# Four small pads that shift tiles within the partition, and three steps moved in a slot table: a fused attention, dense layer and expert router

## Chip, cores and metric
The kernel runs on one core of one Trainium2 chip, as one launch. The metric is the device time of an execution in microseconds (us), the median of several runs.

## What is computed
Linear attention over q, k, v (8 batches, 8 heads, 576 positions, 64 features), a dense layer pair, then a mixture of 8 experts with one expert for each of the 4608 tokens:

```python
q_s = softmax(q, axis=-1); k_s = softmax(k, axis=2)      # k: over the positions
kv  = einsum('bhsd,bhse->bhde', k_s, v)
x   = einsum('bhsd,bhde->bhse', q_s, kv)                 # -> [4608, 512]
h = x @ w_in;  x = (h - tanh(h)) @ w_out                 # 512 -> 2048 -> 512
logits = normed(x) @ normed(expert_emb).T / tau          # 8 experts
e = argmax(logits); gate = softmax(logits)[e]
out = gate * (relu(x @ w1[e]) @ w2[e])                   # 512 -> 1024 -> 512
```

## The kernel before
Work is tiled over tokens in 9 blocks of 512. A block of the dense layers is 16 slots, one for each 128 of the 2048 hidden features, so there are 144 slots. In each slot TensorE (PE) runs 12 matmuls of 512 columns for the first layer (`l1`, line 627, into `hps`) and 12 for the second layer of two slots earlier (`l2`, line 680, into four accumulators `acc`). There are three products for each factor pair, since every fp32 operand is split into a high and a low part: weights `wih`, `wil` (pools `wina`, `winb`) and `woh`, `wol` (pool `wout`), attention output `xth`, `xtl` (pool `xt`), activations `gh`, `gl` (pool `g`). In `l1` the weights are the stationary operand (`lhsT`, loaded by LDWEIGHTS, the rows of PEld) and x streams as the moving operand; in `l2` the activations are stationary and the weights stream.

Between the two, ACT and VectorE (DVE) compute the activation (`gfn`, lines 639 to 641 and 243) and split it (`gsplit`, lines 661 to 665). `hps` has two buffers, so `l1` of a slot needs the first DVE operation of `gfn` (`gg<-hps,gt`) of two slots before.

What else is computed during block j goes into the same slots: k of batch j+1 (class `KUnit`, four pairs of heads p = 0 to 3, each with `mx` the row maxima on DVE, line 363; `red` the maximum over partitions on GpSimd (POOL), line 369, result `mb`; `sub` on DVE, line 381; `exp` on ACT, line 387; `kv` on PE, line 393, result `pk`), q of block j+1 (`QBlock`, lines 543 to 574, partly on POOL as `stq<-stq,...`), and the router of block j-1 (`Router`: logits by 32 DVE products, `soft`, the one-hot `roh`, `rank` on PE at line 787, `fin` on DVE at lines 796 to 819, `scatter` of the rows to DRAM by four DMAs that POOL issues, line 825).

The order on every engine is written out by hand: `at(slot, order, step)` files a step under a slot and a fraction, and `run_slot` emits the steps of a slot by that fraction. Each engine then runs its own instructions in that order, and semaphores between engines do the rest. In a slot, `l1` stands at 0.30, `gfn` at 0.50, `l2` at 0.70, a router product at 0.85, `gsplit` at 0.90. So a step's fraction says what it stands behind on its engine.

After the 144 slots come units of tokens that share an expert: 16 "pair" units of 256 tokens (first layer at line 1131, 96 matmuls of 256 columns each, split as above; second layer at line 1167, 48 matmuls of 512 columns) and then units of 128 tokens.

**Where the tiles lie.** Tiles of a pool lie one behind the other in each partition, in bytes of 4 per fp32 element, and the pools on the left lie one behind the other in the order in which they are opened: `const`, `xt`, `g`, `attn`, `wout`, `wina`. In the built program of before, `const` ends at byte 7072, which is 416 modulo 512. The tiles of `xt` and `g` have sizes that are multiples of 512, so x and the activations start at 416 modulo 512. The tiles of `attn` have not, and the weights of `wout` and `wina` start at 0. The distance of the next stationary operand from the streaming one, modulo 512, is 96 in `l1` and 416 in `l2`. In the expert units the second layer has both operands in one pool, at a distance of 0; in the first layer the distance is 0 in even units (x and weights in the pool `moe2a`, on the right) and 384 in odd ones (x in the pool `moe2b`, on the left).

Of the kernel before, what the change touches and what calls it, by code (L numbers as in the profile page):

```python
# [10 lines left out]
F32 = mybir.dt.float32  # L11
# [10 lines left out]
P = 128  # L22
# [50 lines left out]
def moe_kernel(ctx, tc, q, q_t, k_t, v_t, w_in, w_out, emb, tau, w1, w2, out, dbg=None):  # L73
# [6 lines left out]
    cp = ctx.enter_context(tc.tile_pool(name="const", bufs=1))  # L80
# [4 lines left out]
    pe = nc.tensor  # L85


    ident = cp.tile([P, P], F32, name="ident")
    make_identity(nc, ident)
    ones_b = cp.tile([P, P], BF16, name="ones_b")  # L90
# [61 lines left out]
    def emb_load(xp, gp):  # L152

        em = [
            xp.tile([P, E // 2, DM], F32, name="em0", tag="stl"),
            gp.tile([P, E // 2, DM], F32, name="em1", tag="em1"),
        ]
        for i, z in enumerate(em):
            nc.sync.dma_start(
                out=z.rearrange("p e d -> p (e d)"),  # L160
                in_=emb.rearrange("(o e) d -> o (e d)", o=2)[i : i + 1].to_broadcast(
                    [P, E // 2 * DM]
                ),
            )
        return [em[e // (E // 2)][:, e % (E // 2), :] for e in range(E)]
# [14 lines left out]
    def full_run(general):  # L180
        def lpool(name, **kw):
            st = ExitStack()
            return st, st.enter_context(tc.tile_pool(name=name, bufs=1, reuse_waits="tile", **kw))
# [4 lines left out]
        wos, wop = lpool("wout")  # L188
# [6 lines left out]
        lazy = {}  # L195


        win_h, win_l, wout_h, wout_l = {}, {}, {}, {}
        raws = {}
        npair = [0]  # L200
# [115 lines left out]
        def at(slot, order, fn, *a):  # L316
            ev.setdefault(slot, []).append((order, len(ev.get(slot, ())), fn, a))
# [12 lines left out]
        class KUnit:  # L330
# [84 lines left out]
            def schedule(self, s):  # L415
                if s:
                    at(s - 2, 0.65, self.load)
                    at(s - 2, 0.66, self.loadv)
                    at(s, 0.20, self.mx)
                at(s, 0.30, self.red)  # L420
                at(s + 1, OPT['ks'] if self.b > 1 else OPT['ks1'], self.sub)
                at(s + 1, 0.85, self.exp)
                at(s + 2, OPT['kv'], self.kv)
                at(s + 2, 0.80, self.rs)
                at(s + 3, 0.20, self.out)
# [262 lines left out]
        class Router:  # L688
# [145 lines left out]
            def schedule(self, s):  # L834
                at(s, 0.75, self.evict)
                at(s, 0.98, self.ss, (0, 1))
                at(s + 1, 0.98, self.ss, (2, 3))
                ns = OPT['ns'] if self.j + 2 < NB else (4, 4, 4, 5, 5, 5, 5)
                for i, n in enumerate(ns, 1):
                    at(s + i, 0.22, self.some, n - OPT['gd'])  # L840
                    at(s + i, 0.85, self.some, OPT['gd'])
                s += len(ns)
                at(s, 0.97, self.soft)
                at(s + 1, 0.95, self.rank)
                at(s + 1, 0.97, self.fin)
                at(s + 1, 0.99, self.scatter)


        def make_table(tp, nm, nt, off, cnt, u):
# [428 lines left out]
        def open_router():  # L1278
            ds_.close()
            _, lazy["rp"] = lpool("router", side="right")  # L1280
            lazy["rps"] = _
            lazy["tp"] = lazy["rp"]
            rp = lazy["rp"]
            lazy["em"] = emb_load(xp, rp)
            lazy["ess"] = rp.tile([P, E], F32, name="ess")
            if not general:
                nc.sync.dma_start(out=taub, in_=tau.to_broadcast([P, 1]))

        at(NCH - 1, 0.99, open_router)
        for e in range(E):  # L1290
            at(
# [21 lines left out]
        def x_bufs(pool, n):  # L1313
            lazy["xg"].append(pool.tile([P, 8, P], F32, name=f"xg{n}"))

        def open_second():
            lazy["wbs"].close()
            was.close()
            lazy["sas"], lazy["sa"] = lpool("moe2a", side="right")
            for i in (1, 0):  # L1320
                u0.w1_parts(i)
            lazy["xg"] = []
            x_bufs(lazy["sa"], 0)
            u0.x_parts()
            lazy["w1t"].append(lazy["sa"].tile([P, KD, FF // 2], F32, name="w1t1"))
            u0.loadw1(1)


        u0 = units[0]
        fp = OPT['fp']  # L1330
        at(*OPT['fu'], first_unit)
        at(NS - 1, fp[0], open_second)
        at(NS - 1, fp[1], u0.split1, 0, (0,))
        at(NS - 1, fp[2], u0.split1, 0, (1,))
# [137 lines left out]
    def check(ps_m):  # L1472
# [17 lines left out]
        )  # L1490

    full_run(False)
    fv = nc.values_load(flag[0:1, 0:1], min_val=0, max_val=1)
    with tc.If(fv > 0):
        full_run(True)
# [61 lines left out]
```

## Time and profile before

| | us |
|---|---|
| median of 3 runs (lowest, highest) | 1425.31 (1424.25, 1426.81) |
| the profiled execution, its own time | 1426.07 |
| its span in the trace | 1424.4 |
| PE busy in the span | 1327.9 (93%) |
| DVE busy | 1070.3 (75%) |
| ACT busy | 786.7 (55%) |
| POOL busy | 351.4 (25%) |

An execution's own time is 1.7 us longer than its span. Busy time is the union of an engine's instructions; matmuls overlap in the pipeline, and a matmul of 512 columns has a row of about 0.40 us though the next one starts after 0.23 us. The rate of PE is therefore read from the starts of its rows in the timeline, and its waits from the view of waits.

### The profile page before, as it was taken

What the parts mean: (1) busy time and instruction counts of PE and PEld (TensorE: products, weight loads), DVE (VectorE), ACT (ScalarE), POOL (GpSimd) and SP (SyncE); (2) the same over time, 40 slices, a digit from 0 to 9 for tenths busy, and PEclk for the clock granted to TensorE, in tenths of its full rate; (3) what the DMA queues carried; (4) which work ended last, traced back from release to release, by engine and by line L of the source; (5) the groups of instructions that cost most, each with busy time, mean ns of one, the idle gap of its engine ahead of it and who ended that gap; (6) DMA issues with size and microseconds to landing.
All of it is one profiled execution on the core that took longest, in us unless ns stands there. A gap on an engine that the chain in (4) does not pass through costs nothing. (4 is left out here: it accounts for less than half of the span.)

```text
span 1424.4 us, 20194 instructions
## 1 busy us (share of the span) xinstructions
PE 1327.9 (93%) x6705; PEld 1105.3 (78%) x6705; DVE 1070.3 (75%) x2123; ACT 786.7 (55%) x1567; POOL 351.4 (25%) x335
## 2 busy tenths in 40 slices
PE   3676799999999999999999999999999899999997
PEld 2455677787787787777777787888899799989886
DVE  5788858968869779679689696777997767676453
ACT  3466555554555465564554654546554567676553
POOL 3344511112112112111121220001223343544300
PEclk9888899999999999999999999999999999999998
DMA  5454420121111210210300100005611988847784
GB/s 166 136 158 147 130 70 19 45 71 38 41 57 38 64 53 19 63 53 19 94 22 20 60 1 23 8 23 164 177 38 60 274 296 253 265 127 237 233 309 180
DMA packets 127975, 151.41 MB, mean 106 GB/s; under 512 B 52464, under 2 KB 80624, under 8 KB 127600
## 3 DMA queue, kind: packets, MB, share of 16 engines
q1 hardware_dynamic: 112800, 114.27, 26.4%
q10 hardware_dynamic: 9216, 16.78, 4.1%
q0 software_dynamic: 5840, 18.92, 3.5%
q8 instruction: 57, 0.93, 0.3%
q14 instruction: 62, 0.51, 0.1%
HBM read 164.04 MB, written 23.91 MB: 132 GB/s over the span
## 5 line engine op out<-in xcount | busy, mean ns | idle before, releaser
L680 PE MATMUL acc<-woh,gh 128*128 128x512 f32 x576 | 232.7, 404 | 0.0
L680 PE MATMUL acc<-woh,gl 128*128 128x512 f32 x576 | 229.9, 399 | 0.8 <-DVE gl L665 0.8
L680 PE MATMUL acc<-wol,gh 128*128 128x512 f32 x576 | 229.4, 398 | 0.0
L661 ACT ACTIVATE gh<-gg 128x512 fp32r<-128x512 f32 x144 | 90.9, 631 | 229.2 <-DVE gg L243 227.8
L728 DVE SCALAR_TENSOR_TENSOR rjk<-xr,em 128x512 bf16<-128x512 f32 x288 | 206.3, 731 | 3.1 <-ACT rsq L716 2.9
L627 PE MATMUL hps<-xth,wil 128*128 128x512 f32 x576 | 161.7, 403 | 35.7 <-POOL wil L297 35.7
L627 PE MATMUL hps<-xth,wih 128*128 128x512 f32 x576 | 162.8, 404 | 4.9 <-DVE gg L243 3.6
L627 PEld LDWEIGHTS hps<-xth,wil 128*128 128x128 f32 x576 | 110.3, 192 | 63.5 <-POOL wil L297 37.4
L627 PE MATMUL hps<-xtl,wih 128*128 128x512 f32 x576 | 159.1, 398 | 0.1
L639 ACT ACTIVATE gt<-hps 128x512 f32<-128x512 f32 x144 | 84.7, 588 | 91.1 <-PE hps L627 90.5
L680 PEld LDWEIGHTS acc<-woh,gl 128*128 128x128 f32 x576 | 109.3, 190 | 29.2 <-DVE gl L665 3.0
L680 PEld LDWEIGHTS acc<-woh,gh 128*128 128x128 f32 x576 | 109.8, 191 | 27.2 <-issue 0.7
L680 PEld LDWEIGHTS acc<-wol,gh 128*128 128x128 f32 x576 | 109.3, 190 | 27.6 <-issue 0.8
L627 PEld LDWEIGHTS hps<-xtl,wih 128*128 128x128 f32 x576 | 108.7, 189 | 27.5 <-DVE xtl L613 0.7
L627 PEld LDWEIGHTS hps<-xth,wih 128*128 128x128 f32 x576 | 105.3, 189 | 31.5 <-DVE gg L243 7.2
L243 DVE SCALAR_TENSOR_TENSOR gg<-hps,gt 128x512 f32<-128x512 f32 x144 | 98.1, 681 | 37.4 <-ACT gt L639 26.9
L1167 PE MATMUL po<-wl,hh 128*128 128x512 f32 x296 | 116.3, 393 | 4.2 <-DVE wl L1155 4.2
L1143 DVE SCALAR_TENSOR_TENSOR hl<-ph,hh 128x512 fp32r<-128x512 f32 x74 | 50.9, 688 | 90.7 <-ACT hh L1142 89.7
L243 DVE SCALAR_TENSOR_TENSOR gg<-gy,gg 128x512 f32<-128x512 f32 x144 | 106.2, 737 | 16.1 <-ACT gy L641 0.9
L1167 PE MATMUL po<-wh,hh 128*128 128x512 f32 x296 | 115.9, 392 | 0.0
L1167 PE MATMUL po<-wh,hl 128*128 128x512 f32 x296 | 115.4, 390 | 0.0
L665 DVE TENSOR_TENSOR gl<-gg,gh 128x512 fp32r<-128x512 f32 x132 | 95.4, 722 | 25.0 <-ACT gh L661 23.8
(266 smaller groups left out, 2527.5 us busy)
## 6 DMA issues: line engine op xcount, KB each, us to landing
w2t<-in_moe_w_dram SPq DMA_DIRECT2D x84, 512.0 KB
w1t<-in_w_t_dram SPq DMA_DIRECT2D x38, 1024.0 KB
vt<-in_v_t_dram SPq DMA_DIRECT2D x32, 325.0 KB
kt<-in_k_t_dram SPq DMA_DIRECT2D x56, 160.0 KB
gw<-in_moe_w_in_dram ACTq DMA_DIRECT2D x32, 256.0 KB
gw<-in_moe_w_out_dram ACTq DMA_DIRECT2D x32, 256.0 KB
xg<-xs_d SPq DMA_DIRECT2D x60, 128.0 KB
stq<-in_q_t_dram SPq DMA_DIRECT2D x14, 512.0 KB
```

Of the source, the lines that this page charges most:

```text
L243: dve.scalar_tensor_tensor(out=o, in0=x, scalar=s1, in1=y, op0=op0, op1=op1)
L627: pe.matmul(h, lhsT=wt[:, kk, :], rhs=xx[:, kk, :], start=(n == 0), stop=(n == 3 * KD - 1),)
L639: act(out=t, in_=h, func=AF.Square)
L661: act(out=gh, in_=g, func=AF.Copy)
L665: e.tensor_tensor(out=gl, in0=g, in1=gh.bitcast(F32), op=ALU.subtract)
L680: pe.matmul(acc[j, t], lhsT=a[:, sl], rhs=r, start=(c == 0 and i == 0), stop=(c == NCH - 1 and i == 2),)
L728: dve.scalar_tensor_tensor(out=jk, in0=self.x[t // 2][:, t % 2, 0:DM], scalar=1.0, in1=lazy["em"][e], op0=ALU.mult, op1=ALU.mult, accum_ou ...
L1143: dve.scalar_tensor_tensor(out=hl, in0=self.ph, scalar=0.0, in1=hh.bitcast(F32), op0=ALU.max, op1=ALU.subtract,)
L1167: pe.matmul(po, lhsT=a[:, f % self.wd, sl], rhs=r[:, f % 2, :], start=(f == 0 and i == 0), stop=(f == 7 and i == 2),)
```

## The change
Four tiles are allocated that nothing writes or reads: 32 bytes at the start of `const`, 416 bytes at the start of `wout`, 32 bytes at the start of the router's pool (on the right), and 192 and 320 bytes in `moe2a`, on the right. And three kinds of steps get other places: for batches 2 to 8, `mx` goes from fraction 0.20 of its slot to 0.80 of the slot before, and `red` from 0.30 to 0.01; `rank`, `fin` and `scatter` go from 0.95, 0.97 and 0.99 of a slot to 0.32, 0.33 and 0.34 of the next, which is behind that slot's `l1`.

```diff
+    cp.tile([P, 8], F32, name="pad0")
     ident = cp.tile([P, P], F32, name="ident")
...
+        wop.tile([P, 104], F32, name="pad1")
         win_h, win_l, wout_h, wout_l = {}, {}, {}, {}
...
                     at(s - 2, 0.65, self.load)
                     at(s - 2, 0.66, self.loadv)
-                    at(s, 0.20, self.mx)
-                at(s, 0.30, self.red)
+                    late = self.b < 2
+                    at(s if late else s - 1, 0.20 if late else 0.80, self.mx)
+                at(s, 0.30 if self.b < 2 else 0.01, self.red)
...
                 at(s, 0.97, self.soft)
-                at(s + 1, 0.95, self.rank)
-                at(s + 1, 0.97, self.fin)
-                at(s + 1, 0.99, self.scatter)
+                at(s + 2, 0.32, self.rank)
+                at(s + 2, 0.33, self.fin)
+                at(s + 2, 0.34, self.scatter)
...
             rp = lazy["rp"]
+            rp.tile([P, 8], F32, name="pad2")
             lazy["em"] = emb_load(xp, rp)
...
             x_bufs(lazy["sa"], 0)
+            lazy["sa"].tile([P, 48], F32, name="pad3")
             u0.x_parts()
             lazy["w1t"].append(lazy["sa"].tile([P, KD, FF // 2], F32, name="w1t1"))
             u0.loadw1(1)
+            lazy["sa"].tile([P, 80], F32, name="pad4")
```

In the built program, x and activations of the dense layers now start at 448 modulo 512, and so do their weights (0 + 32 + 416): the distance is 0 in `l1` and in `l2`. The second layer of the expert units stays at 0. In their first layer x is at 448 and the split weights are at 256, so the distance is 320 in all pair units.

On PE, near the end of a block, the rank product (`pr`, with its two weight loads) stood ahead of a slot's `l1`. Before:

```order
L393 MATMUL pk<-vt,kt 128x130 x5
L787 LDWEIGHTS tri
L787 MATMUL pr<-roh,tri 128x32
L787 LDWEIGHTS ones_b
L787 MATMUL pr<-roh,ones_b 128x32
L627 MATMUL hps<-xth,wih_1178 128x512 x4
L627 MATMUL hps<-xtl,wih_1178 128x512 x4
L627 MATMUL hps<-xth,wil_1179 128x512 x4
```

After the change:

```order
L396 MATMUL pk<-vt,kt 128x130 x5
L631 MATMUL hps<-xth,wih_1180 128x512 x4
L631 MATMUL hps<-xtl,wih_1180 128x512 x4
L631 MATMUL hps<-xth,wil_1181 128x512 x4
L791 LDWEIGHTS tri
L791 MATMUL pr<-roh,tri 128x32
L791 LDWEIGHTS ones_b
L791 MATMUL pr<-roh,ones_b 128x32
```

It moved behind the twelve matmuls of `l1`; on DVE the order of `soft` and `fin` among their neighbours is unchanged.

On POOL, over a block; `ISA mb<-mx` is the maximum over partitions, and a bare `ISA` is a change of POOL's program library between it and the `TENSOR_TENSOR` rows. Before:

```order
L369 ISA mb<-mx 128x128
L703 COPY xr<-tokid 128x2 x2
L566 ISA
L566 TENSOR_TENSOR stq<-stq,qbmax 128x512 x2
L369 ISA
L369 ISA mb<-mx 128x128
L566 ISA
L566 TENSOR_TENSOR stq<-stq,qbmax 128x512 x2
L566 TENSOR_TENSOR stq<-stq,qbadd 128x512 x2
L369 ISA
L369 ISA mb<-mx 128x128
```

After the change:

```order
L372 ISA mb<-mx 128x128
L707 COPY xr<-tokid 128x2 x2
L372 ISA mb<-mx 128x128
L570 ISA
L570 TENSOR_TENSOR stq<-stq,qbmax 128x512 x4
L570 TENSOR_TENSOR stq<-stq,qbadd 128x512 x2
L372 ISA
L372 ISA mb<-mx 128x128
```

The maximum of pair p = 1 moved ahead of the four subtractions of q, and two changes of library are gone from each such block.

On DVE, in the slot of pair p = 2's maxima. Before:

```order
L562 RECIPROCAL qbadd<-qbadd 128x64
L728 SCALAR_TENSOR_TENSOR rjk,rl<-xr,em_1414 128x512
L665 TENSOR_TENSOR gl<-gg,gh 128x512
L363 TENSOR_REDUCE mx<-kt 128x128
L728 SCALAR_TENSOR_TENSOR rjk,rl<-xr,em_1414 128x512
```

After the change:

```order
L566 RECIPROCAL qbadd<-qbadd 128x64
L366 TENSOR_REDUCE mx<-kt 128x128
L732 SCALAR_TENSOR_TENSOR rjk,rl<-xr,em_1417 128x512
L669 TENSOR_TENSOR gl<-gg,gh 128x512
L732 SCALAR_TENSOR_TENSOR rjk,rl<-xr,em_1417 128x512
```

The reduction moved two rows up, ahead of a router product and of the split of the activation.

## Rows read from the trace of the kernel before
**Rows 1.** The windows view (us, busy of each engine with instruction counts, clock, DMA share, GB/s).
```profile
0.00:165.00 165.00, 99.88 (x416) 77.89 (x417) 128.83 (x191) 81.90 (x212) 70.97 (x76) 0.85 0.48 147
...
560.00:986.00 426.00, 418.67 (x1833) 333.71 (x1832) 329.07 (x804) 227.91 (x480) 62.62 (x66) 1.00 0.14 41
986.00:1414.00 428.00, 423.83 (x2747) 385.91 (x2745) 303.84 (x419) 257.62 (x397) 140.29 (x119) 1.00 0.66 208
```

**Rows 2.** The same view for line 627 alone (PE and PEld).
```profile
165.00:986.00 821.00, 387.69 (x1562) 290.66 (x1560) 1.00 0.16 46
```

**Rows 3.** The view of waits on PE (us in total, times, longest).
```profile
PE hps L627 <- POOL wil L297: 35.7, 4, 10.3
...
PE pr L787 <- DVE roh L778: 9.4, 6, 1.7
...
PE hps L627 <- DVE gg L243: 3.6, 7, 1.0
PE pk L393 <- ACT kt L387: 3.2, 8, 0.9
```

**Rows 4.** Timeline of PE, one slot (start us, us, engine, line, operation, tiles, shape, count).
```profile
408.82 1.08 PE L627 MATMUL hps<-xth,wih 128*128 128x512 f32 x4
...
411.61 0.40 PE L680 MATMUL acc<-woh,gh 128*128 128x512 f32 x1
...
414.42 0.40 PE L627 MATMUL hps<-xth,wih 128*128 128x512 f32 x1
```

**Rows 5.** Timeline of PE, second layer of a pair unit of the experts.
```profile
1019.68 0.40 PE L1167 MATMUL po<-wh,hh 128*128 128x512 f32 x1
...
1021.75 0.39 PE L1167 MATMUL po<-wh,hh 128*128 128x512 f32 x1
...
1030.60 0.64 PE L1131 MATMUL ph<-xth,w1h 128*128 128x256 f32 x4
```

**Rows 6.** Timeline of PE, first layer of two pair units: end of an even one, start of an odd.
```profile
1042.12 0.39 PE L1167 MATMUL po<-wh,hh 128*128 128x512 f32 x1
...
1008.15 0.53 PE L1131 MATMUL ph<-xth,w1h 128*128 128x256 f32 x3
```

**Rows 7.** Timeline around the rank product, PE and DVE.
```profile
474.33 1.28 PE L393 MATMUL pk<-vt,kt 128*128 128x130 f32 x10
...
476.92 0.19 DVE L778 TENSOR_TENSOR roh<-rca,rcm 128x32 bf16<-128x32 f32 x1
...
477.17 0.19 PE L787 MATMUL pr<-roh,tri 128*128 128x32 bf16 x1 [1.56 <-DVE roh L778]
...
480.02 0.17 DVE L796 COPY rrb<-rrb 128x8 f32<-128x8 f32 x1
```

**Rows 8.** Timeline around two of k's pairs: POOL, DVE, PE.
```profile
423.73 0.72 POOL L369 PARTITION_ALL_REDUCE mb<-mx  x1 [5.71 <-issue]
...
439.53 2.76 POOL L566 TENSOR_TENSOR stq<-stq,qbadd 128x512 f32<-128x512 f32 x2 [5.67 <-DVE qbadd L562]
448.20 0.72 POOL L369 PARTITION_ALL_REDUCE mb<-mx  x1 [5.91 <-issue]
...
424.48 0.83 DVE L381 TENSOR_TENSOR kt<-kt,mb 128x640 f32<-128x640 f32 x1 [3.12 <-POOL mb L369]
...
426.13 1.39 PE L393 MATMUL pk<-vt,kt 128*128 128x130 f32 x10 [0.34 <-ACT kt L387]
...
450.60 1.38 PE L393 MATMUL pk<-vt,kt 128*128 128x130 f32 x10 [0.17 <-ACT kt L387]
```

**Rows 9.** Timeline of a wait for a first-layer accumulator: DVE, PE.
```profile
443.81 0.68 DVE L243 SCALAR_TENSOR_TENSOR gg<-hps,gt 128x512 f32<-128x512 f32 x1
...
444.55 1.21 PE L627 MATMUL hps<-xth,wih 128*128 128x512 f32 x4 [0.21 <-DVE gg L243]
```

**Rows 10.** Timeline of the next block's first pair: exponential on ACT, product on PE.
```profile
499.01 0.72 ACT L387 ACTIVATE kt<-kt 128x640 f32<-128x640 f32 x1
...
503.16 1.28 PE L393 MATMUL pk<-vt,kt 128*128 128x130 f32 x10
```


## Prediction
> **What bounds the kernel now.** I read the windows first. From 165 to 1414 us PE is the bound: in the stretches of the dense layers and of the experts it is busy for 418.67 of 426 and 423.83 of 428 us, while DVE is at 329 and 304 us, and the granted clock is 1.00 in both [rows 1]. So a nanosecond saved on PE there is a nanosecond of the run, and work of other engines counts only where PE waits for it. Before 165 us it is not so: PE is busy for 99.88 of 165 us, and four waits for decoded weights, 35.7 us in all, set the pace [rows 1, 3]. What PE saves there is waited away.
>
> Next I read how fast PE goes where it never waits. The 12 matmuls of a slot's `l1` start at 408.82 us, the 12 of `l2` at 411.61, the next slot's at 414.42: 2.79/12 = 232.5 ns and 2.81/12 = 234.2 ns for one, 5.60 us for the 24 [rows 4]. The second layer of an expert unit, with the same shapes and the same clock, does 48 in 1030.60 - 1019.68 = 10.92 us: 227.5 ns for one; its first nine take 2.07 us (230 ns), the other 39 take 8.85 us (226.9 ns) [rows 5]. Something makes each matmul of the dense layers 5 to 7 ns slower than the shape demands.
>
> Then the waits of PE. Beyond the decode they are short but regular: 9.4 us in 6 times for the one-hot ahead of the rank product, 3.6 us for the accumulator of `l1`, 3.2 us for k's exponential [rows 3].
>
> **The change part by part.**
>
> *Distances in the dense layers.* What differs between the two rates is where the operands lie: 96 and 416 in the dense layers, 0 in the experts' second layer. The change makes all of them 0. In the stretch where PE sets the pace, line 627 has 1562 recorded matmuls, which is 130 slots of 12 [rows 2]. If a slot's 24 matmuls go at 227.5 ns, they take 5.46 instead of 5.60 us, 0.14 us less: 130 x 0.14 = 18.2 us. The ends: at the 230 ns of the first nine after a break, a slot takes 5.52 us and the gain is 130 x 0.08 = 10.4 us; at 226.9 ns it takes 5.45 us, and the gain is 130 x 0.154 = 20.0 us. Dense slots have breaks too (a new accumulator every three matmuls in `l2`, k's product in one slot of four); the run of 48 has its break in its mean, so I take its 227.5 ns. As the nearest row that speaks against it: its DVE is a little less busy (71 against 77% of the stretch [rows 1]).
>
> [...]
>
> *Distances in the experts' first layer.* An even unit (distance 0) does 96 matmuls of 256 columns from 1030.60 to 1042.12 us, an odd one (384) from 1008.15 to 1019.68: 120.0 and 120.1 ns for one [rows 5, 6]. No row has 320. Bounds: the only price of a distance that rows show is the 6.7 ns between 234.2 and 227.5 [rows 4, 5]; on the 1536 matmuls of the 16 pair units that is 10.3 us, either way. Two distances that far apart read alike, so I take 0.
>
> *The rank product.* It waits at the head of PE, so all twelve matmuls of the next `l1` queue behind it. In the block shown, k's product ends at 474.33 + 1.28 = 475.61 us, `roh` starts at 476.92, and the product at 477.17: 1.56 us idle [rows 7]. Behind the twelve matmuls, 2.8 us later, `roh` has long been done, and its operands are all that it waits for; the wait goes: 9.4 us in the 6 blocks that show it [rows 3]. The product itself costs PE the same in both places. Queued behind it is `fin` on DVE, which starts at 480.02 us [rows 7]; with `l1` starting at 475.6, the product is done by about 478.5, so `fin` and the four scatter DMAs that POOL issues after it don't move. What is late next: in the new order PE is 1.6 us ahead of DVE, POOL and the scatter. The nearest deadline is the next block's first pair, whose maximum stands behind the scatter on POOL: its exponential is done at 499.01 + 0.72 = 499.73 and PE asks for it at 503.16 [rows 10]. Of this slack of 3.4 us the change uses 1.6 and, by four faster slots, 0.6. It holds.
>
> *k's maxima.* `mx` costs DVE the same and passes two or three instructions, all of them ahead of the same `gg<-hps,gt`; so the 3.6 us that PE waits for that one [rows 3, 9] stay, give or take a microsecond. `red` is another matter for p = 1. Before, it needs a change of POOL's library between the subtractions of q: POOL idles for 5.71 us ahead of it, `sub` starts at 424.48, and PE idles for 0.34 us ahead of its `pk` at 426.13 [rows 8]. Ahead of the subtractions it runs as soon as `mx` is done, and that wait goes: 2.1 us, two thirds of the 3.2 (the p = 2 waits show 0.17 us each [rows 8]). For p = 2 the library change stays (5.91 us before 448.20 [rows 8]), behind the products of q that end a chain on DVE; faster slots bring PE there sooner: 2.7 slots x 0.14 = 0.38 us more of a wait in each of about 6 blocks, 2.2 us. The two cancel. I count 0, with 3 us either way.
>
> *The other distances* (decode, the expert weights' splits on DVE) lie beside PE's work and change by nanoseconds: 0.
>
> **The sum.** 18.2 + 9.4 + 0 + 0 = 27.6 us. From the profiled execution's 1426.07 us that gives 1398.5; its own time lies 0.8 us above the median of the runs, 1425.31, so for the median 1397.7, said as **1398 us**.
>
> **The rivals.**
>
> 1. [...] Chance 0.10.
>
> 2. *320 is a dear distance.* Every matmul of the experts' first layer pays the 6.7 ns: 1398 + 10.3 = 1408 us. For it: 96 and 416 are dear in the dense layers. Against it: 384 isn't, at this width [rows 6]. Chance 0.10.
>
> 3. *DVE takes PE's place after the rank product.* From `soft` to `fin` DVE has little idle time (476.92 to 480.02 holds `roh`, the next `gg` and a split [rows 7]); PE, 1.6 us ahead, then waits for `gg` or for the operand of `l2` and gives the 9.4 us back: 1398 + 9.4 = 1407 us. Against it: two buffers of `hps` give PE two slots of grace. Chance 0.10.
>
> 4. *Zero is the dear distance (slower).* The weight load and the stream begin together; if it is the equal start that makes them collide, and the experts' second layer is fast for another reason, each dense matmul pays the 5.8 ns instead of saving them: 1425.3 + 18.2 - 9.4 = 1434 us. It turns slower from 9.4/130 = 0.072 us a slot, 3 ns a matmul. Against it: the only long run at 0 is the fastest of this shape in the trace [rows 5]. Chance 0.04.
>
> **How the numbers follow.** The forecast has 0.66. Its own range is 1398 - 1.8 (226.9 ns) - 3 - 4 (less than half of the 10.3 us downward) = 1389 to 1398 + 7.8 (230 ns) + 3 = 1409. Rivals 2 and 3 (1408, 1407) lie in it, and 2 us on top take in that one of them meets a smaller gain; rivals 1 and 4 (0.14) and the tails of the forecast (0.06) are left out: 1389 to 1411 us. A measurement of this kernel can tell some 0.2%, 2.9 us, from no change. Faster by more than that are the forecast and rivals 1 to 3, 0.96, less 0.01 for a case in which rival 1 and rival 3 come together and nothing is left: 0.95, same 0.01, slower 0.04.
>
> **What would show it.** Right: a slot's `l1` starts 5.46 us after the last one's, and the mean rows of lines 627 and 680 come down to those of line 1167 (the new line numbers are 4 higher); no wait of PE for `roh`; on POOL the p = 1 maximum ahead of the four subtractions; 96 matmuls of the first expert layer in 11.5 us in odd and even units. Wrong: slots still of 5.60 us (rival 1) or longer (rival 4); the first expert layer off 120 ns (rival 2, or a gain that I don't count); PE waiting for `gg`, `gl` or `kt` by some 10 us more than before (rival 3).

## The result and the profile after

The changed kernel takes 1393.18 us (median of 4 runs, 1387.9 to 1394.0); the kernel before, beside it, 1425.68 us. The ratio is 0.9765 (95% interval 0.9739 to 0.9791): 32.5 us faster, where 27.6 were forecast. The profiled execution is the shortest of the four, 1387.9 us with a span of 1386.2.

The windows of the kernel after, cut where its experts begin, answer to [rows 1] (same columns):

```profile
0.00:165.00 165.00, 99.19 (x417) 78.62 (x418) 129.61 (x191) 81.75 (x212) 71.45 (x76) 0.87 0.48 147
560.00:951.00 391.00, 387.67 (x1739) 318.10 (x1738) 310.23 (x756) 216.83 (x461) 64.36 (x65) 1.00 0.14 43
951.00:1376.00 425.00, 420.48 (x2748) 382.39 (x2746) 302.84 (x420) 258.45 (x398) 141.10 (x119) 1.00 0.66 209
```

Up to 165 us nothing changed. The experts begin at 951 instead of 986 us and take 425 instead of 428 us. PE still bounds the stretch before them (387.67 of 391 us), but DVE is now at 310 of 391, 79%.

The timeline of PE, one dense slot, beside [rows 4]:

```profile
401.93 1.07 PE L631 MATMUL hps<-xth,wih 128*128 128x512 f32 x4
...
404.65 0.39 PE L684 MATMUL acc<-woh,gh 128*128 128x512 f32 x1
...
407.37 1.07 PE L631 MATMUL hps<-xth,wih 128*128 128x512 f32 x4
```

`l1` and `l2` take 2.72 us each, 226.7 ns a matmul, and the slot 5.44 us instead of 5.60. The same view in the experts, an odd unit and then an even one, beside [rows 5, 6]:

```profile
973.13 0.64 PE L1135 MATMUL ph<-xth,w1h 128*128 128x256 f32 x4
...
984.44 0.40 PE L1171 MATMUL po<-wh,hh 128*128 128x512 f32 x1
...
995.35 0.63 PE L1135 MATMUL ph<-xth,w1h 128*128 128x256 f32 x4
...
1006.65 0.40 PE L1171 MATMUL po<-wh,hh 128*128 128x512 f32 x1
```

The 96 matmuls of the first layer take 11.31 and 11.30 us, 117.8 ns each, where 120.0 was read before; the second layer (10.91 us for 48) did not change. Now the waits of PE, beside [rows 3]:

```profile
PE hps L631 <- POOL wil L300: 38.0, 4, 10.6
...
PE acc L684 <- DVE gl L669: 5.1, 3, 3.3
...
PE hps L631 <- DVE gg L246: 1.3, 2, 1.1
...
PE pk L396 <- ACT kt L390: 0.5, 1, 0.5
```

The wait for `roh` is gone, as forecast. Those for `gg` (3.6) and `kt` (3.2) are nearly gone too, which was not. And there is a new one, 3.3 us for `gl`, whose place the timeline of all engines shows:

```profile
926.92 0.97 POOL L829 DMA_INDIRECT xs_d<-xr,rrow  x1 [3.83 <-DMA xs_d<-xr,rrow]
...
927.91 0.14 POOL L923 MEMSET Aco<- 1x9 int32 x2
...
928.00 0.19 DVE L884 TENSOR_TENSOR Adv<-Aval 1x8 f32<-1x8 f32 x1 [9.90 <-POOL Aco L923]
...
929.88 0.67 DVE L669 TENSOR_TENSOR gl<-gg,gh 128x512 fp32r<-128x512 f32 x1
...
930.61 0.50 PE L684 MATMUL acc<-woh,gl 128*128 128x512 f32 x1 [3.33 <-DVE gl L669]
...
931.72 0.63 PE L684 MATMUL acc<-woh,gl 128*128 128x512 f32 x1
```

`make_table` lets POOL fill the first expert table `A` with constants. On POOL's queue these memsets stand behind the four scatters of the last router piece, which now come later than the table's steps on DVE. DVE stands still for 9.90 us, with `gl` behind it, and PE waits for `gl` (before: 6.9 us on DVE, and no wait of more than 0.4 us for `gl` on PE). Then seven matmuls start 0.43 us apart instead of 0.23. The windows view shows why:

```profile
930.50:934.50 4.00, 3.89 (x10) 3.07 (x11) 2.69 (x9) 1.84 (x5) 0.11 (x1) 0.57 0.19 49
934.50:945.00 10.50, 10.50 (x47) 8.68 (x47) 6.57 (x10) 6.44 (x12) 0.00 (x0) 1.00 0.52 142
```

Behind the wait the granted clock is 0.57 over 4 us, 0.50 from 932 to 934 us; then it is back at 1.00. The wait and the slow matmuls cost 3.3 + 7 x 0.2 = 4.7 us.

### The profile page after: what moved, and what is told of

Its sections match the earlier page's. It is cut to its first block, busy times and chain, and to the rows that moved or that the text cites. A ratio compares the mean times of both kernels' runs of the same rounds, so it can differ in the third digit from the quotient of the medians.

```text
span 1386.2 us, 20164 instructions
## 1 busy us (share of the span) xinstructions
PE 1299.2 (94%) x6705; PEld 1101.9 (79%) x6705; DVE 1072.3 (77%) x2123; ACT 784.7 (57%) x1567; POOL 358.5 (26%) x335
## 3 DMA queue, kind: packets, MB, share of 16 engines
q1 hardware_dynamic: 112800, 114.27, 26.9%
## 5 line engine op out<-in xcount | busy, mean ns | idle before, releaser
L684 PE MATMUL acc<-woh,gl 128*128 128x512 f32 x576 | 226.8, 394 | 5.1 <-DVE gl L669 5.1
L732 DVE SCALAR_TENSOR_TENSOR rjk<-xr,em 128x512 bf16<-128x512 f32 x288 | 209.6, 742 | 7.4 <-ACT rsq L720 7.2
L631 PE MATMUL hps<-xth,wil 128*128 128x512 f32 x576 | 158.2, 397 | 38.0 <-POOL wil L300 38.0
L631 PE MATMUL hps<-xth,wih 128*128 128x512 f32 x576 | 158.6, 397 | 3.0 <-ACT wih L298 1.7
L631 PE MATMUL hps<-xtl,wih 128*128 128x512 f32 x576 | 154.6, 390 | 0.0
L631 PEld LDWEIGHTS hps<-xtl,wih 128*128 128x128 f32 x576 | 108.1, 188 | 23.4 <-DVE xtl L617 0.4
L669 DVE TENSOR_TENSOR gl<-gg,gh 128x512 fp32r<-128x512 f32 x132 | 99.7, 755 | 21.4 <-ACT gh L665 20.3
```

The costliest lines, as they stand in the source:

```text
L631: pe.matmul(h, lhsT=wt[:, kk, :], rhs=xx[:, kk, :], start=(n == 0), stop=(n == 3 * KD - 1),)
L669: e.tensor_tensor(out=gl, in0=g, in1=gh.bitcast(F32), op=ALU.subtract)
L684: pe.matmul(acc[j, t], lhsT=a[:, sl], rhs=r, start=(c == 0 and i == 0), stop=(c == NCH - 1 and i == 2),)
L732: dve.scalar_tensor_tensor(out=jk, in0=self.x[t // 2][:, t % 2, 0:DM], scalar=1.0, in1=lazy["em"][e], op0=ALU.mult, op1=ALU.mult, accum_ou ...
```

## The experiments

Every ratio is against runs of the kernel before on the same chip (its medians there: 1428 to 1430 us). "Us gained" is (1 - ratio) x 1425.7; an interval is 2 to 3 us either way. "Half clock" counts the dense matmuls that start 0.40 to 0.48 us apart, in rows of three or more, between 175 us and the experts. In the experts the granted clock also fell once, for 6.8 us, in nine of the twelve profiled executions (not in those of the kernel before, of the changed kernel's first run and of the pads alone); between the two traces of the changed kernel the experts differ by 2.4 us, one with this fall and one without.

| pads | rank | k's maxima | ratio (95%) | us gained | waits for roh, kt, gg, gl | half clock |
|---|---|---|---|---|---|---|
| no | no | no | 1 | 0 | 9.4, 3.2, 3.6, 0.8 | 0 |
| yes | no | no | 0.998 (0.9966 to 0.9994) | 2.9 | 13.9, 6.0, 4.8, 2.1 | 44 |
| no | yes | no | 0.995 (0.9936 to 0.9964) | 7.1 | 0, 2.8, 2.5, 3.5 | 13 |
| no | no | yes | 0.9917 (0.99 to 0.9934) | 11.8 | 4.5, 0.2, 0.7, 2.0 | 0 |
| yes | yes | no | 0.9836 (0.9817 to 0.9854) | 23.4 | 0, 5.5, 3.9, 3.8 | 8 |
| yes | no | yes | 0.9866 (0.9848 to 0.9884) | 19.1 | 13.0, 0, 1.1, 3.0 | 20 |
| no | yes | yes | 0.9883 (0.9865 to 0.9901) | 16.7 | 0, 0, 0.6, 4.4 | 8 |
| yes | yes | yes | 0.9763 (0.9743 to 0.9783) | 33.8 | 0, 0, 1.9, 5.5 | 6 |

The three parts alone bring 2.9 + 7.1 + 11.8 = 21.8 us; together they bring 33.8. The runs one by one:

### The pads alone

The change has five pads (32, 416, 32, 192 and 320 bytes), not four as the title and the text on the change say.

```diff
+    cp.tile([P, 8], F32, name="pad0")
...
+        wop.tile([P, 104], F32, name="pad1")
...
+            rp.tile([P, 8], F32, name="pad2")
...
+            lazy["sa"].tile([P, 48], F32, name="pad3")
...
+            lazy["sa"].tile([P, 80], F32, name="pad4")
```

> The kernel before with the five pads alone; no step is moved. Theory 1 (TensorE pays for the distance modulo 512 bytes between its two operands): every dense matmul of 512 columns goes to the 227.5 ns that the kernel before shows at distance 0, and the 130 slots between router and experts lose 0.14 us each as forecast, or 0.15 to 0.16 as the changed kernel's trace has them; with the experts' first layer (1536 matmuls from 120.0 to 117.6 ns, 3.7 us) that is 18 to 24 us, so 1401 to 1407 us, while the wait for roh (9.4 us) and those for gg and kt (3.6 and 3.2 us) stand as before. Rival 1 (the distance decides nothing and the whole gain is that of the moved steps): matmuls stay at 233 to 235 ns and the time at 1425 us.

Theory 1 was right about the matmuls, and the rival came near the time, but not for its reason. The matmuls did go to 227 ns (median distance of starts, in all six groups of the dense layers; 232 to 235 before): summed over the some 3120 with a record, 18.7 us. The time hardly moved. Waits of PE:

```profile
PE pr L790 <- DVE roh L781: 13.9, 6, 2.5
PE pk L396 <- ACT kt L390: 6.0, 12, 1.4
PE hps L630 <- DVE gg L246: 4.8, 8, 1.1
```

They are 24.7 us against 16.2 before. And the timeline of PE around one rank product:

```profile
271.63 1.28 PE L396 MATMUL pk<-vt,kt 128*128 128x130 f32 x10
275.44 0.19 PE L790 MATMUL pr<-roh,tri 128*128 128x32 bf16 x1 [2.53 <-DVE roh L781]
275.48 0.18 PE L790 MATMUL pr<-roh,ones_b 128*128 128x32 bf16 x1
275.50 1.31 PE L630 MATMUL hps<-xth,wih 128*128 128x512 f32 x4
276.61 1.91 PE L630 MATMUL hps<-xtl,wih 128*128 128x512 f32 x4
```

In the 10 us ahead the windows view has DVE (the third busy time) at 9.79 us, in the kernel before and in this run:

```profile
262.00:272.00 10.00, 10.00 (x47) 8.16 (x46) 9.79 (x25) 4.37 (x9) 0.97 (x1) 1.00 0.00 1
```

```profile
262.00:272.00 10.00, 10.00 (x48) 8.29 (x47) 9.79 (x23) 4.30 (x8) 0.97 (x1) 1.00 0.01 2
```

DVE brings `roh` when it can, and a faster PE only waits longer. Behind the wait the same view has, in this run:

```profile
275.50:278.30 2.80, 2.80 (x10) 2.19 (x11) 2.23 (x6) 2.00 (x5) 0.00 (x0) 0.66 0.42 127
```

The same stretch of the kernel before, behind a wait of 1.5 us, has a clock of 1.00:

```profile
274.20:277.00 2.80, 2.80 (x14) 2.30 (x15) 2.23 (x6) 2.01 (x5) 0.00 (x0) 1.00 0.85 217
```

So each of six blocks loses a longer wait and seven or eight matmuls at half clock, 44 in all. The account: 18.7 us from dense matmuls and 3.7 from the experts' first layer, less 8.5 of these waits, 1.3 more for `gl` and 44 x 0.2 = 8.8 of half clock, leaves 3.8 us; the runs say 2.9 (0.9 to 4.8).

### The rank product alone

```diff
-                at(s + 1, 0.95, self.rank)
...
+                at(s + 2, 0.32, self.rank)
...
```

> The kernel before with the rank product, its end and the scatter at their new places alone; no pads, k's maxima as before. Theory 1: the six waits for roh (9.4 us) are gone and nothing comes in their place, so 1416 us; dense matmuls stay at 233 to 235 ns. Theory 2 (read from the changed kernel's trace): the last scatter now holds POOL's queue in front of the first table's memsets, TensorE waits some 3 us for gl and its granted clock falls to half for some 3 us behind it, so only 4 to 6 us are left, 1419 to 1421. Rival 3 (VectorE takes TensorE's place as the bound): 1425.

Theory 2, though 7.1 us is a little above its 4 to 6. The waits for `roh` are gone, but the new wait for the table is there:

```profile
PE acc L680 <- DVE gl L665: 3.5, 3, 3.0
```

### k's maxima alone

```diff
-                    at(s, 0.20, self.mx)
-                at(s, 0.30, self.red)
+                    late = self.b < 2
+                    at(s if late else s - 1, 0.20 if late else 0.80, self.mx)
+                at(s, 0.30 if self.b < 2 else 0.01, self.red)
```

> The kernel before with k's row maxima and their reduction at the new places alone; no pads, the rank product as before. Theory 1 (the forecast): the wait of the first k pair falls by what the others grow, 0 with ends at 3 us either way, 1422 to 1428 us. Theory 2 (read from the changed kernel's trace, where the waits for kt fell from 3.2 to 0.5 us and those for gg from 3.6 to 1.3): both are the work of this move, 5 us less, 1420.

More than either theory: 11.8 us. The waits of PE say that this move also helps where none of its steps stands, at the rank product:

```profile
PE pr L788 <- DVE roh L779: 4.5, 5, 1.8
...
PE hps L628 <- DVE gg L243: 0.7, 1, 0.7
...
PE pk L393 <- ACT kt L387: 0.2, 1, 0.2
```

So it gives DVE time for the whole rest of the block. The next pairs tell which time.

### The three pairs, and the change once more

> The pads and the moved rank product together; k's maxima as before. The run with the pads alone had its dense matmuls at 227 ns and gained only 3 us: the six waits for roh grew from 1.6-1.9 to 2.2-2.7 us and the granted clock was at half for 7 or 8 matmuls behind each. Theory 1 (the pads' gain was lost in these waits, as VectorE's steps in the last slots of a block set when roh comes): with the rank product moved, both are gone, and pads and rank together bring what the forecast gave them, 18 + 9.4 to 22 + 9.4 us, 1.9 to 2.2% of the time before (ratio 0.978 to 0.981). Theory 2 (VectorE sets the pace of the whole block while k's maxima are at their old places, wherever the rank product stands): the waits turn up for kt and gg instead, each growing from 3 to over 8 us, and the two bring 11 to 15 us (ratio 0.989 to 0.992).

The ratio, 0.9836, lies between the theories. The waits for `roh` and the clock falls behind them are gone, and the pads' time comes through with them: 23.4 us for two parts that bring 10.0 one by one. What Theory 2 feared is there in part:

```profile
PE pk L396 <- ACT kt L390: 5.5, 10, 0.8
...
PE hps L630 <- DVE gg L246: 3.9, 8, 0.7
```

> The pads and the moved k maxima together; the rank product as before. Theory 1: shorter matmuls let TensorE come to the rank product sooner than VectorE has roh, so the waits for roh grow from the 4.5 us of the run with the maxima alone to 8 to 14 us, with the half granted clock behind those of 2.2 us and more; the two bring 13 + 18 less 5 to 15 us, ratio 0.982 to 0.989. Theory 2 (k's maxima at their old places were what held VectorE back): the waits for roh stay at 4 to 5 us and the two bring all of 13 + 18 us or more, ratio 0.978 or less.

Theory 1: `roh` is waited for again (13.0 us in six times), and behind three of the six the clock fell.

> The two moves without the pads; dense matmuls at 233 to 235 ns. The moves brought 8.0 and 12.8 us alone and share the waits for roh (9.4 us before, 4.5 with the maxima alone, none with the rank product moved). Theory 1: 12.8 + 4.5 less what the wait for the first expert table takes back (3 us and a clock fall), 13 to 17 us, ratio 0.988 to 0.991; the change's other 15 to 20 us are then the pads', worth their forecast once nothing waits for VectorE. Rival (the moves bring most of the change's 33 us): ratio 0.982 or less.

Theory 1. The pads on top of the two moves are then worth 33.8 - 16.7 = 17.1 us, near the 18.2 forecast for them.

> The changed kernel once more, beside the three pairs of parts. Theory 1: ratio 0.974 to 0.979 as in its first comparison, TensorE's wait for gl near 927 us 3 to 3.5 us long with the half granted clock behind it, and the profiled execution 3 to 5 us slower than that of the kernel with the first table's memsets on VectorE (1388.6 median). Rival (the fast profiled execution of 1387.9 us is the usual one and the 1393 of the others a disturbance): median 1388 to 1389, and the table's move brought nothing.

Theory 1: 1397.0 us, ratio 0.9763, and the wait for `gl` again (5.5 us, the longest 3.9, over the 3 to 3.5 that were expected). The profiled execution is 8.4 us above the median with the memsets on DVE, not 3 to 5. The 1387.9 us of the first profile was mostly a short start: its dense stretch was under way 5.0 us earlier than in this one, counted at the same slot; from there to the experts the two differ by 1.5 us. In the experts they differ by 2.4 us: this execution spends 6.8 us at half clock behind a wait of 2.34 us for `wl` (at 1086.6 us), and the first one, behind a wait of 2.35 us, none. What makes the start differ from run to run was not tried.

### One half of the maxima's move

To the kernel with pads and rank, the place of `mx` alone was added; `red` stays at 0.30:

```diff
-                    at(s, 0.20, self.mx)
+                    late = self.b < 2
+                    at(s if late else s - 1, 0.20 if late else 0.80, self.mx)
                 at(s, 0.30, self.red)
```

> Pads and moved rank product, and of the move of k's maxima one half: mx runs earlier on VectorE, but its reduction over partitions (red, on POOL) stays behind the subtractions of q. Theory 1 (POOL's order decides: VectorE stands still at the subtraction of kt for some 3.3 us a block until POOL's mb is there, and what is queued behind it, gg first, is late for the rest of the block): the idle time of VectorE ahead of kt<-kt,mb stays at 50 to 57 us as in the kernel with pads and rank alone (38 in the changed kernel), TensorE's waits for kt and gg stay at 5.5 and 3.9 us, and the time at the ratio of that kernel, 0.982 to 0.985. Theory 2 (the 1.3 us of mx on VectorE ahead of gg is what makes gg late): the waits for gg go to some 1 us and the ratio comes to 0.976 to 0.979, that of the changed kernel.

Ratio 0.9881 (0.9861 to 0.9901): moving `mx` alone is worse than not moving it, by some 6 us. Theory 2 is out. Theory 1 has its main point: the idle time of DVE stayed, as the view of the tile `mb` (who waited for it: us, times) shows for this run,

```profile
  DVE kt L384: 60.3, 17
```

for the kernel with pads and rank,

```profile
  DVE kt L384: 61.2, 17
```

for the changed kernel,

```profile
  DVE kt L384: 39.2, 11
```

and for the kernel before:

```profile
  DVE kt L381: 55.3, 17
```

Only `red` takes the six away. This run and the changed kernel differ by `red` alone: (0.9881 - 0.9763) x 1425.7 = 16.8 us. What Theory 1 missed is the harm, in the timeline of DVE and the waits of PE:

```profile
421.12 0.82 DVE L384 TENSOR_TENSOR kt<-kt,mb 128x640 f32<-128x640 f32 x1 [3.31 <-POOL mb L372]
...
435.92 1.23 DVE L366 TENSOR_REDUCE mx<-kt 128x128 f32<-128x640 f32 x1
...
437.68 1.52 DVE L669 TENSOR_TENSOR gl<-gg,gh 128x512 fp32r<-128x512 f32 x1
```

```profile
PE acc L684 <- DVE gl L669: 10.6, 7, 2.8
PE pk L396 <- ACT kt L390: 7.4, 6, 1.7
```

After the 3.31 us DVE has no idle time up to `mx`, and `mx` (1.23 us) now stands ahead of `gl`. The row of `gl` also takes 1.52 us there, as one row a block does in the kernel before too. In five blocks PE waits 1.0 to 1.5 us for it. In the changed kernel the order is the same and rows of 1.52 us are there too, but PE's waits for `gl` are 5.5 us in all, 3.9 of them at the table; that this is so because DVE isn't behind is argued from the idle time. There the pair's maximum is ready long before its subtraction, which starts without a wait:

```profile
402.27 0.99 POOL L372 PARTITION_ALL_REDUCE mb<-mx  x1 [14.04 <-DVE mx L366]
...
409.19 0.82 DVE L384 TENSOR_TENSOR kt<-kt,mb 128x640 f32<-128x640 f32 x1
```

### A version that beats both

The changed kernel with the first table's memsets on DVE:

```diff
-            nc.gpsimd.memset(val[:, ng : ng + 1], 1e6)
+            (dve if nm == "A" else nc.gpsimd).memset(val[:, ng : ng + 1], 1e6)
...
-                nc.gpsimd.memset(co[d], 1)
+                (dve if nm == "A" else nc.gpsimd).memset(co[d], 1)
```

> The changed kernel with the memsets of the first expert table on VectorE instead of POOL, nothing else. Theory 2 (these memsets stand on POOL's queue behind the four scatters of the last router piece, and VectorE, then TensorE, wait for them): VectorE's 9.9 us of idle time ahead of the table's first use of them is gone, and with it TensorE's 3.5 us wait for gl at 927 us and the half granted clock behind it, so 3 to 6 us under the changed kernel's 1393, 1387 to 1390. Rival (VectorE would wait there for something else of the table, or its own extra work takes the place): the wait stays at over 3 us, 1393.

1388.57 us, ratio 0.9714 (0.9698 to 0.9731), against 0.9763 and 0.9765 for the changed kernel: 0.5% (7 us, give or take 4) less. The waits of PE, and DVE at the table:

```profile
PE acc L684 <- DVE gl L669: 1.8, 2, 1.6
```

```profile
921.61 0.15 DVE L884 TENSOR_TENSOR Adv<-Aval 1x8 f32<-1x8 f32 x1
```

There is no idle time ahead of it, and no dense matmul at half clock after 175 us. One stretch at half clock is left, in the experts, behind a wait of 2.35 us for `wl`:

```profile
1080.00:1086.80 6.80, 5.25 (x13) 3.59 (x13) 6.65 (x16) 4.51 (x5) 0.98 (x1) 0.50 1.05 336
```

### Sixteen distances in one run

```diff
-        wop.tile([P, 104], F32, name="pad1")
...
+            pool.tile([P, 8], F32, name=f"pad{nm}{c}")
...
-            lazy["sa"].tile([P, 48], F32, name="pad3")
...
-            lazy["sa"].tile([P, 80], F32, name="pad4")
```

> The changed kernel with a pad of 32 bytes ahead of every pair of weight tiles in place of one pad ahead of all, and without the two pads in the experts' pool: the dense matmuls run through all sixteen distances from 0 to 480 bytes in steps of 32 within one run, the experts' first layer at 0 in even units and 320 in odd ones. Theory 1 (the distance modulo 512 decides, whatever the addresses are): 227 ns a matmul at 0, 233 to 235 at 96 and at 416 as in the kernel before, the others between 227 and 240; the 256-column matmuls 120.0 ns at 0 and 117.6 at 320. Theory 2 (only two operands at the same address modulo 512 gain): 227 at 0 alone and 233 to 235 everywhere else. Rival 1 (the places do not matter by themselves; the matmuls ran at 227 ns for another reason): no dependence on the pair, all at one value. No time is forecast beyond that it lies between that of the changed kernel and 18 us above.

Two slots' first layers from the timeline, at a distance of 256 and of 416 (the row of `acc` is the start of what follows the twelve matmuls, so 2.73 and 2.81 us, 227.5 and 234.2 ns a matmul):

```profile
410.61 1.08 PE L631 MATMUL hps<-xth,wih 128*128 128x512 f32 x4
...
413.34 0.39 PE L684 MATMUL acc<-woh,gh 128*128 128x512 f32 x1
...
440.07 1.09 PE L631 MATMUL hps<-xth,wih 128*128 128x512 f32 x4
...
442.88 0.39 PE L684 MATMUL acc<-woh,gh 128*128 128x512 f32 x1
```

The mean distance of starts within a slot, in ns, worked out from the trace after 175 us, starts 300 ns and more apart left out (80 to 108 for each entry; next stationary against streaming operand, modulo 512):

```
distance    0     32    64    96    128   160   192   224
l1        228.4 232.6 233.3 234.3 233.0 233.5 230.4 233.0
l2        229.7 233.4 233.3 233.6 233.0 233.1 230.0 233.2
distance  256   288   320   352   384   416   448   480
l1        227.9 232.6 233.4 234.2 232.6 234.5 230.5 233.1
l2        229.1 233.9 233.3 233.5 233.3 233.4 229.9 232.6
```

Theory 1: the period follows the distance, in one run, with the streaming operand of `l1` always at 448. It isn't that address that counts: in the experts' second layer both operands are at 416 in the kernel before and at 448 in the changed one, at one rate (10.92 and 10.91 us for 48). As each distance has its own slot of a block, the slot could be the cause; but the kernel before, where all sixteen slots have one distance, has means of 232.9 to 234.7 in them, and the changed kernel 226.6 to 227.6, or up to 230.2 in slots that come right behind products of another shape. `l1` at 64, 192, 320 and 448 is such a slot: 192 and 448 have 230.4 and 230.5 there, where the changed kernel at 0 has 230.1 and 229.6, so it stays open whether they are worse than 0; 64 and 320 are worse by 3 to 4 ns. Theory 2 is out in its "0 alone": 256 is as good as 0, and 192 and 448 come next; the two rows repeat after 256 bytes. Why, no run here shows. In runs of one distance it is 227.7 and 227.1 ns at 0, and 233.8 at 96 and 416. The 256-column matmuls of even units (0) have 120.0 ns, those of odd ones (320) 117.7, so the width matters: 0, the best for 512 columns, isn't for 256. The run took 1411.39 us (one execution; the kernel before beside it 1428.84), 16 us less of a gain than the changed kernel's, inside what was expected.

## Why the prediction was right, and where it was wrong

**Distances in the dense layers: right.** 18.2 us forecast, 18.7 in the matmuls, 17.1 as the last part added. Rival 1, that the distance does nothing, counts with 0.10 in the chances and is refuted: no run shows it, and with weights at 96 bytes from the stream a matmul starts some 6 ns later than at 0 (233.8 and 227.7 ns). Why, no run shows either. But the step "a nanosecond saved on PE there is a nanosecond of the run" failed: alone, the pads brought 2.9 us. It rested on busy shares of stretches [rows 1], in which DVE looks 77% busy. In the last slots before each rank product it had no time left, and there it set the pace. That is akin to rival 3 (DVE in PE's place), but at another point: with the pads, PE waits 13.9 and 13.0 us for `roh` where the rank product stayed, and 9.4 us for `kt` and `gg` where only the maxima stayed. In the full change these waits are 1.9 us.

**The experts' first layer: mis-sized.** 0 was taken, 1536 x 2.4 ns = 3.7 us was gained, inside the bounds. Rival 2 had the wrong sign.

**The rank product: right in its wait, short in what it protects.** Its 9.4 us went. Beside the faster matmuls the same wait would have been 13 to 14 us with the half clock behind it; the product's move is worth 33.8 - 19.1 = 14.7 us there. The step that looked for what is late next checked k's pair behind the scatter on POOL and overlooked the table's memsets behind the last scatter: 4.7 us lost.

**k's maxima: wrong.** 0 with 3 us either way was said; on top of the other two they bring 33.8 - 23.4 = 10.4 us. The step that failed is the price of `red` by what PE waits for `kt`. The row itself was there [rows 8]: ahead of `kt<-kt,mb` DVE stood still for 3.12 us, waiting for POOL's `mb`, and what queues behind it in order (router products, the next `gg`) was late. With the maxima alone moved, this idle time fell from 55.3 to 38.2 us, and with it PE's waits for `gg` and `kt` from 6.8 to 0.9 us and those for `roh` from 9.4 to 4.5. "The 3.6 us stay" looked at the order of `mx` and `gg`, and the run with `mx` alone shows that this order was not the cause. That step also priced at nothing that `mx` passes `gl`: with `red` late, PE waits 10.6 us for `gl`, against 3.8 with `mx` at its old place.

**The sum.** PE's account in the profiled execution: matmuls 18.7 + 3.7, waits for `roh`, `kt` and `gg` from 16.2 to 1.8 us (14.4), less 4.3 more for `gl` and 1.4 of half clock: 31.1 us. The medians differ by 32.5, but the two profiled executions by 38.2 (1426.07 and 1387.9). Of the missing 7.1 us, 1.7 lie in the start (the same slot begins at 209.0 and 207.3 us), and 2.9 between the starts of k's products (26.9 us before, 24.0 after); why these are shorter was not looked for, and 2.5 us stay open. The forecast's 27.6 lacked the maxima's wait times and the experts' 3.7 us, and the table's loss offset part of it. Pads and rank product together brought 23.4 us where 27.6 were forecast, the maxima 10.4 where 0 was: two errors of opposite sign, so it is partly luck that the time came out so near.

## What to carry to other kernels

An in-order engine that waits early in a block can make another engine wait much later, at an operand that has nothing to do with it (with the maxima alone moved, DVE's idle time ahead of `kt` fell from 55.3 to 38.2 us, and PE's waits for `roh` from 9.4 to 4.5): before costing a wait by the last engine in line, look for idle time on the engine that delivers, and count everything queued behind. A saving on the bounding engine counts only up to the next engine's own finish at each meeting point (18.7 + 3.7 = 22.4 us off the matmuls, 2.9 off the run with the pads alone), so look at busy shares in the 10 us before a wait, not over hundreds. And when a step moves on a queue, list what stands behind its last instance too, where the program goes on to something else (the table's memsets here, 4.7 us).

## What was not expected of the hardware

- In the mixed run the matmul period at 512 columns went with the distance between next weights and stream, and its values repeated after 256 bytes: some 228 to 230 ns at 0, 230 at 192 (in slots where 0 can have 230 too), 232.6 to 234.5 elsewhere.
- At 256 columns the order was another: 120.0 ns at 0 and 120.1 at 384 in the kernel before [rows 5, 6], 117.7 at 320 in the mixed run.
- Some waits of PE cost twice. Behind the waits of 3 us and more for the table, and behind all six of 2.0 to 2.5 us in the run of the pads, the granted clock fell for six to thirteen matmuls, 0.2 us more for each; behind those of up to 1.8 us for `roh` it stayed at 1.00. Between them it is not regular: of the six of 2.1 to 2.3 us in the run of pads and maxima, three had it, and of the waits of 1.9 to 2.4 us for `wl` in the experts, one in each of the twelve profiled executions, nine.
